# Attention in pairs of heads: where in the load queue a pair's values and the reciprocals of its sums stand

## The chip, the cores and the metric

The kernel runs on one core of a Trainium2 chip. The metric is the device time of one execution in microseconds (us), from the first to the last instruction and a little around them. The core has a matrix engine (TensorE, in the profile PE, its weight loads PEld), three elementwise engines (VectorE = DVE, ScalarE = ACT, GpSimd = POOL) and a sync engine (SP) that does nothing but issue transfers (DMAs). Each engine works through its own list of instructions in order. An instruction that waits for a semaphore holds up everything behind it on the same engine. That is also so on SP: a transfer that may not start yet holds up every later one.

## What is computed

Three layers follow one another; only the first is touched here.

```python
# B, H, S, D = 2, 8, 576, 64
scores = scale * np.matmul(q, k.transpose(0, 1, 3, 2))
...
bias = h @ w2                                   # a small net of the distance of two positions, one value per head
scores = scores + bias.transpose(2, 0, 1)[None, :, :, :]
scores = scores - np.max(scores, axis=-1, keepdims=True)
attn = np.exp(scores)
attn = attn / (np.sum(attn, axis=-1, keepdims=True) + 1e-09)
return np.matmul(attn, v).astype(np.float32)
# then  x = relu-like maximum of three products, times w_out   (1152 x 512 x 768)
# then  a mixture of 8 experts with balanced weights            (1152 x 512 x 1024 each)
```

## The kernel before

The program has these stages, in this order: the bias stage (0 to 70 us of the span), attention (68 to 216 us), the first product layer (the loop with `m1_mm`, to 326 us), then the experts to the end at 1082 us.

**Bias stage.** The bias of every head, row and column goes through a tensor in DRAM (`bias_f`). A loop over 36 groups `g16` of 16 rows makes each group on PE and DVE (`bias_mm`, `bias_ev`, `bias_out`), in one of six buffers `bo`, and `bias_store` writes it to DRAM. So the store of group n must have landed before `bias_out` of group n + 6 writes the buffer again. Behind groups 12, 20 and 28 `load_bias(0)` to `load_bias(2)` fetch the first bias tiles back, in the layout that attention wants.

**Attention.** The eight heads are taken in four pairs `p` (0 to 3), and a pair in nine steps `k` (0 to 8); step `s = 9p + k` of 36 handles 128 rows of queries of both heads `x`. In a step `u_qk` makes the scores on PE, `u_max` (L452, DVE, once per head) adds the bias tile and finds the row's extreme, `u_exp` (ACT) makes the exponentials and their sums, `u_tr` and `u_ev` transpose them (PE, then ACT and DVE). The product with the values, `pv_mm`, runs later: table `PV` gives pair p its parts at steps 9p + 5 to 9p + 13. A pair's values are therefore still read in the fifth step (k = 4) of the next pair, and first read in the sixth step (k = 5) of its own.

**The transfers of a pair.** All of them are issued by SP through the helper `dma` (L59), in the order in which the loop over `s` (L590 to L624) calls them:

- `load_pair(p + 1)` at k = 1: queries and keys of the next pair (two transfers of 576 KB into `qk`), then its values (640 KB into `v`). Both tiles have two buffers. The values of pair p + 1 go where those of pair p - 1 lie, and these are read by PE up to k = 4 of pair p.
- `load_bias(n)` at even k, with n = 5p + k/2 + 2: the bias tiles of both heads for row block n % 5 of pair n // 5, 288 KB each. There are six buffers, so tile n goes where tile n - 3 lay, which is read for the last time one step earlier. The tiles loaded at k = 2 (n = 5p + 3) are wanted by `u_max` at k = 6, those of k = 4 at k = 8, those of k = 6 and k = 8 at k = 0 and 2 of the next pair.
- the reciprocals of the sums: `r_add` at k = 0 forms them (DVE), `r_tr` and `r_out` at k = 1 write them to DRAM (`r_d`), `r_in` at k = 2 reads them back, spread over the partitions (four transfers, 576 KB in all, one buffer). `x_out` (POOL, called at k = 6 and 7) multiplies the finished rows of the pair before by them.
- `load_item`: weights of the first product layer, 512 KB each; `w_step` prepares them with DVE, ACT and POOL instructions spread over the steps `W_AT` of pairs 1 to 3.

In the source, `r_in` stands ahead of `load_bias` in a step, and `load_pair` behind it.

Of the kernel before, what the change touches and what calls it, by code (L numbers as in the profile page):

```python
# [9 lines left out]
F32 = mybir.dt.float32  # L10
# [10 lines left out]
B, H, S, D = 2, 8, 576, 64  # L21
# [30 lines left out]
def make_body(stop=None):  # L52
    def body(tc, a):
# [4 lines left out]
        def dma(out, in_):  # L58
            nc.sync.dma_start(out=out, in_=in_)  # L59
# [7 lines left out]
        def pool(name, bufs=1, space=None, side=None):  # L67
            kw = {}
            if space is not None:
                kw["space"] = space  # L70
            if side is not None:
                kw["side"] = side
            return tc.tile_pool(name=name, bufs=bufs, **kw)

        with ctx, tc.manual_schedule():
# [92 lines left out]
            hp_ = hctx.enter_context(pool("heads", bufs=2))  # L168

            qk_t, v_t = {}, {}  # L170
            bias_t = {}

            def load_pair(p):
                if p < H // 2:
                    qk_t[p] = hp_.tile([128, 2, B, S], F32, tag="qk", name="qk")
                    v_t[p] = hp_.tile([128, 2, B, 5, D], F32, tag="v", name="v")
                    for part in range(2):
                        dma(qk_t[p][:, part], a["qk"][p][:, part])
                    dma(v_t[p], a["v"][p])

            def load_bias(n):

                p, it = divmod(n, 5)
                for h in range(2 * p, 2 * p + 2) if n < 5 * H // 2 else ():
                    t = hp_.tile([128, S], F32, tag="bias", name="bias", bufs=6)
                    if it < 4:
                        dma(t, bias_d[128 * it:128 * it + 128, h, :])
                    else:
                        for e in range(2):
                            dma(t[64 * e:64 * e + 64], bias_d[512:576, h, :])  # L190
                    bias_t[h, it] = t


            with ExitStack() as bctx:
# [7 lines left out]
                dma(par, a["par"])  # L202
                nc.scalar.dma_start(out=rr, in_=a["tab4"])
                dma(tab16, a["tab16"])
                load_pair(0)
                w1r, b1r, w2r, msk, c4, wb1, w2a = (
                    par[:, i:j] for i, j in ((0, 1), (1, 2), (2, 10), (10, 42), (42, 186), (186, 250), (250, 506)))
                l16, ic16 = tab16[:, :TW], tab16[:, TW:]
# [20 lines left out]
                v, kf, po = (eu[:, i] for i in range(3))  # L229
# [77 lines left out]
                def gen_s(g):  # L307


                    n = width(g // 4)  # L310
                    s = sp.tile([128, 3, 194], F16, tag="s", name="s")[:, :, :n // 3]
                    win = v3(window(rs, g // 4))
                    kind = TESTS0[g] if g < len(TESTS0) else (TESTSL if g // 4 == NG16 - 1 else TESTS)[g % 4]
                    if kind == "A":
                        A.activation(out=s, in_=win, func=AF.Sigmoid, bias=nthr[:, g:g + 1], scale=STEEP)
                    else:
                        eng = G if kind == "G" else V
                        eng.tensor_scalar(out=s, in0=win, scalar1=thr[:, g:g + 1], scalar2=None, op0=ALU.is_gt)
                    s_t[g] = s
# [12 lines left out]
                def bias_mm(g16):  # L332
                    ps = []
                    for q in range(2):
                        pt, sls = sums(pb[q].tile([128, 2, 512], F32, tag="p", name="p"), width(g16))
                        ps.append(pt)
                        for p in range(2):
                            for sl in sls:
                                for c in range(4):
                                    T.matmul(out=pt[32 * c:32 * c + 32, sl, :], lhsT=wb[p][:, q, :],  # L340
                                             rhs=s_t[4 * g16 + c][:, sl, :], start=(p == 0), stop=(p == 1))
                    for c in range(4):
                        del s_t[4 * g16 + c]
                    return ps

                def bias_ev(g16, ps):
                    n = width(g16)
                    t = ev.tile([128, S], F32, tag="t", name="t")[:, :n]
                    V.scalar_tensor_tensor(out=v3(t), in0=ps[0], scalar=ics[:, g16:g16 + 1], in1=v3(window(l16, g16)),
                                           op0=ALU.mult, op1=ALU.mult)  # L350
                    return t
# [3 lines left out]
                def bias_out(g16, ps, t):  # L355
                    n = width(g16)
                    bo = bo_t[g16] = ev.tile([128, S + 24], F32, tag="bo", name="bo", bufs=6)
                    o = 16 * g16 + 15 if side(g16)[1] else 0
                    V.scalar_tensor_tensor(out=v3(bo[:, o:o + n]), in0=ps[1], scalar=sc[:, 1:2], in1=v3(t),  # L359
                                           op0=ALU.mult, op1=ALU.add)  # L360
# [17 lines left out]
                for g16 in range(NG16):  # L378
                    ps = bias_mm(g16)
                    t = bias_ev(g16, ps)  # L380
                    for c in range(4):
                        if g16 + 2 < NG16:
                            gen_s(4 * (g16 + 2) + c)
                    bias_out(g16, ps, t)
                    if g16 == NG16 - 1:

                        A.activation(out=bc.tile([128, 1], F32, name="ex"), in_=ones[:, 0:1], func=AF.Exp)
                    for n in range(max(g16 - 1, 0), NG16 if g16 == NG16 - 1 else g16):
                        bias_store(n)
                    if g16 in (12, 20, 28):  # L390
                        load_bias((12, 20, 28).index(g16))

            if stop == "bias":
                with pool("dbg") as dp:
# [15 lines left out]
            with ExitStack() as actx:  # L410
# [74 lines left out]
                def r_in(p):  # L485

                    r_t[0] = up.tile([128, B, S], F32, tag="r", name="r", bufs=1)
                    for x in range(2):
                        dma(r_t[0][half[x], :, 0:512], r_d[p, 9 * x:9 * x + 8, :].rearrange(
                            "(b t) p -> b (t p)", b=B).unsqueeze(0).to_broadcast([64, B, 512]))  # L490
                        dma(r_t[0][half[x], :, 512:576], r_d[p, 9 * x + 8, :].rearrange(
                            "(b p) -> b p", b=B).unsqueeze(0).to_broadcast([64, B, 64]))

                def u_tr(u, x):

                    pe = un[u]["pe"][x]
                    pt = un[u]["pt"] = ps_t.tile([128, 2, 512], F32, tag="pt", name="pt")
                    for j in range(5):
                        c = min(128 * j, S - 128)
                        for i in range(2):  # L500
                            T.transpose(pt[:, i, 64 * j:64 * j + 64], pe[half[i], c:c + 128], ident[half[i], half[i]])  # L501
# [76 lines left out]
                def in_turn(table, s):  # L578

                    return [(p, table[s - 9 * p]) for p in range(NP) if s - 9 * p in table]  # L580
# [9 lines left out]
                for s in range(NU):  # L590
                    p, k = divmod(s, 9)
                    u_qk(s)
                    if s > 0:
                        u_tr(s - 1, 0)
                    pv_part(s)
                    for x in range(2):
                        u_max(s, x)
                    if s > 0:
                        u_ev(s - 1, 0)
                    u_exp(s, 0)  # L600
                    for n, e in in_turn(EV, s):
                        pv_ev(n, *e)
                    u_exp(s, 1)
                    if s > 0:
                        u_tr(s - 1, 1)
                        u_ev(s - 1, 1)
                    if s > 8:
                        if k == 0:
                            r_add(p - 1)
                        if k == 1:  # L610
                            r_out(p - 1)
                        if k == 2:
                            r_in(p - 1)
                        if k in (6, 7):
                            x_out(p - 1, k - 6)
                        if k in W_AT:
                            w_step(last=2)
                    if s in (3, 7):
                        load_item(s // 4)
                    if s > 0 and (k == 0 or k % 2 == 0) and 5 * p + k // 2 + 2 < 5 * NP:  # L620
                        load_bias(5 * p + k // 2 + 2)
                    if k == 1:
                        load_pair(p + 1)
                    un.pop(s - 2, None)  # L624

                u = NU - 1
# [126 lines left out]
            with ExitStack() as mctx:  # L753
# [216 lines left out]
                for n, g in enumerate((0, 2, 1, 3)):  # L970
                    for d in range(4):
                        k = 4 * n + d
                        p = (ps_o, ps_o, ps_m, ps_m)[d].tile([128, 512], F32, tag="oomm"[d] + "2", name="o")
# [333 lines left out]
```

## Time and profile before

| | before |
|---|---|
| time, median of 3 runs | 1082.54 us (1078.12 to 1086.18) |
| profiled execution | 1084.35 us, of which 1082.6 us are the span |
| PE busy | 1049.3 us, 97% of the span |
| DVE, ACT, POOL busy | 755.8, 561.0, 313.3 us (70, 52, 29%) |
| mean granted TensorE clock | 0.984 of full speed |
| transfers of SP's queue | 83.81 MB, 27.2% of the 16 DMA engines' time |

The profile is of one execution. A busy share near 100% for PE does not say that nothing is lost: matmuls at a lower granted clock take longer and count as busy all the same, and a few us of waiting are well under 1% of the span. What the change is worth is read from the attention stage alone, from the queue of SP and from the engines that wait for its transfers.

### The profile page before, as it was taken

How to read it: one execution, taken by the hardware profiler on the slowest of the kernel's cores; microseconds unless marked ns; L12 is line 12 of the kernel's file. 1: busy time of each engine (PE TensorE's matmuls, PEld its weight loads, DVE VectorE, ACT ScalarE, POOL GpSimd, SP SyncE). 2: the span in 40 equal slices, each digit the busy share in tenths (PEclk: the TensorE clock that was granted, in tenths of full speed). 3: DMA queues.
4: the chain of work that ended last, by engine and by line, in shares of the span. 5: the costliest groups of instructions: out<-in, count | busy, mean ns of one | idle time of the engine just before them, and what ended most of it. 6: DMA issues, size and time to landing. Idle time of an engine off the chain costs nothing.

```text
span 1082.6 us, 18890 instructions
## 1 busy us (share of the span) xinstructions
PE 1049.3 (97%) x7533; PEld 686.5 (63%) x7533; DVE 755.8 (70%) x1464; ACT 561.0 (52%) x922; POOL 313.3 (29%) x227
## 2 busy tenths in 40 slices
PE   7989889999999999999999999999999999999998
PEld 3245455699999765665756657557566575665753
DVE  7977556599977877877667576676775666757543
ACT  6967566544434576454544545454445454454530
POOL 6830211322224224135141331322413314133120
PEclk8989898999999999999999999999999999999999
DMA  5884655243414013022130230211302203010002
GB/s 178 257 258 115 172 159 139 73 156 118 102 40 154 22 42 83 21 64 47 38 84 21 64 74 31 64 35 50 83 20 64 58 26 83 21 45 6 1 1 88
DMA packets 39446, 85.31 MB, mean 79 GB/s; under 512 B 8053, under 2 KB 10301, under 8 KB 39357
## 3 DMA queue, kind: packets, MB, share of 16 engines
q1 hardware_dynamic: 39212, 83.81, 27.2%
q8 instruction: 59, 0.97, 0.4%
q10 hardware_dynamic: 144, 0.29, 0.1%
q14 instruction: 31, 0.25, 0.1%
HBM read 70.78 MB, written 13.30 MB: 78 GB/s over the span
## 4 chain that ended last, share of the span: by engine, by line
PE 84%; DVE 9%; ACT 3%; DMA 3%; issue 1%; POOL 0%; SPq 0%; DVEq 0%; ACTq 0%
PE d L1211 32%; PE x L1126 12%; PE m L560 10%; PE y L1126 8%; PE z L1126 8%; PE pv L529 3%; PE sc L435 3%; PE pt L501 3%; PE p L340 2%; DVE bo L359 1%; DMA bias<-bias_f 1%; PE o L977 1%; DVE hl L1149 1%; DVE s L1140 1%; DVE pk L704 1%
## 5 line engine op out<-in xcount | busy, mean ns | idle before, releaser
L1211 PE MATMUL d<-w2h,hh 128*128 128x512 f16 x576 | 218.3, 379 | 0.8 <-DVE acc L1222 0.8
L1211 PE MATMUL d<-w2h,hl 128*128 128x512 f16 x576 | 218.3, 379 | 0.2 <-DVE hl L1149 0.2
L1211 PE MATMUL d<-w2l,hh 128*128 128x512 f16 x576 | 218.3, 379 | 0.0
L1126 PEld LDWEIGHTS <-w1h 128*128 128x128 f16 x1792 | 175.5, 98 | 49.8 <-issue 2.3
L1211 PEld LDWEIGHTS <-hh 128*128 128x128 f16 x1152 | 112.6, 98 | 132.9 <-issue 1.0
L1225 DVE SCALAR_TENSOR_TENSOR acc<-d,kh,acc 128x512 f32<-128x512 f32 x126 | 94.3, 748 | 93.7 <-PE d L1211 93.6
L857 POOL TENSOR_TENSOR w1l<-wf,w1h 128x768 f16<-128x768 f32 x32 | 53.6, 1677 | 360.2 <-ACT w1h L856 286.0
L1144 ACT ACTIVATE hh<-s 128x576 f16<-128x576 f32 x128 | 87.3, 683 | 128.6 <-DVE s L1140 100.9
L1149 DVE SCALAR_TENSOR_TENSOR hl<-s,hh 128x576 f16<-128x576 f32 x128 | 99.2, 777 | 48.4 <-ACT hh L1144 45.9
L863 POOL TENSOR_TENSOR w1l<-wf,w1h 128x1024 f16<-128x1024 f32 x32 | 68.8, 2152 | 117.6 <-ACT w1h L860 117.6
L860 ACT ACTIVATE w1h<-wf 128x1024 f16<-128x1024 f32 x32 | 33.8, 1056 | 132.5 <-DVE wf L853 132.5
L1126 PEld LDWEIGHTS <-w1l 128*128 128x128 f16 x896 | 87.9, 98 | 22.8 <-issue 0.4
L1211 PEld LDWEIGHTS <-hl 128*128 128x128 f16 x576 | 56.4, 98 | 68.5 <-DVE hl L1149 0.7
L1136 ACT ACTIVATE s<-x,cx 128x576 f32<-128x576 f32 x96 | 70.3, 733 | 27.0 <-PE x L1126 26.6
L938 POOL TENSOR_TENSOR w2l<-w2r,w2h 128x512 f16<-128x512 f32 x64 | 73.1, 1159 | 25.0 <-ACT w2h L937 25.0
L1126 PE MATMUL x<-xth,w1h 128*128 128x288 f16 x384 | 78.5, 286 | 0.6 <-ACT s L1136 0.6
L1126 PE MATMUL x<-xtl,w1h 128*128 128x288 f16 x384 | 78.6, 286 | 0.2 <-POOL xtl L868 0.2
L1126 PE MATMUL x<-xth,w1l 128*128 128x288 f16 x384 | 78.5, 286 | 0.0
L1140 DVE SCALAR_TENSOR_TENSOR s<-z,cx,s 128x576 f32<-128x576 f32 x64 | 52.3, 818 | 32.0 <-PE z L1126 25.6
L560 PE MATMUL m<-xh,wh 128*128 128x384 f32 x216 | 72.7, 337 | 0.0
L560 PE MATMUL m<-xl,wh 128*128 128x384 f32 x216 | 72.5, 336 | 0.1
L560 PE MATMUL m<-xh,wl 128*128 128x384 f32 x216 | 72.4, 335 | 0.0
(203 smaller groups left out, 1990.3 us busy)
## 6 DMA issues: line engine op xcount, KB each, us to landing
wr<-in_moe_w SPq DMA_DIRECT2D x50, 512.0 KB, 3.6
w2r<-in_moe_w SPq DMA_DIRECT2D x64, 256.0 KB, 2.9
bias_f<-bo SPq DMA_DIRECT2D x36, 295.5 KB, 3.6
bias<-bias_f SPq DMA_DIRECT2D x32, 288.0 KB, 4.6
qk<-in_qk SPq DMA_DIRECT2D x8, 576.0 KB, 5.8
wr<-in_moe_w_out SPq DMA_DIRECT2D x6, 512.0 KB, 4.1
v<-in_v SPq DMA_DIRECT2D x4, 640.0 KB, 4.3
bias<-bias_f SPq DMA_DIRECT2D x16, 144.0 KB, 5.8
```

Of the source, the lines that this page charges most:

```text
L560: T.matmul(out=p[:, :TG], lhsT=ws[:, 128 * c:128 * c + 128], rhs=xs[:, c, TG * g:TG * g + TG], start=(c == 0 and n == 0), stop=(c == 3 and ...
L857: G.tensor_tensor(out=lo[:, 0:3], in0=t[:, 1:4], in1=hi[:, 0:3], op=ALU.subtract)
L860: A.activation(out=hi[:, 3:7], in_=t[:, 4:8], func=AF.Copy)
L863: G.tensor_tensor(out=lo[:, 3:7], in0=t[:, 4:8], in1=hi[:, 3:7], op=ALU.subtract)
L938: G.tensor_tensor(out=lo, in0=r, in1=hi, op=ALU.subtract)
L1126: T.matmul(out=ps[bank][:, s, :SH], lhsT=ws[:, i, c, :], rhs=xv[:, j, c, s * SH:s * SH + SH], start=(start and k == 0), stop=(k == 5), **kw)
L1136: A.activation(out=t, in_=src, func=AF.Identity, scale=c)
L1140: V.scalar_tensor_tensor(out=out, in0=z, scalar=scale, in1=out, op0=ALU.mult, op1=ALU.add)
L1144: A.activation(out=o, in_=src, func=AF.Relu)
L1149: V.scalar_tensor_tensor(out=l, in0=src, scalar=0.0, in1=o, op0=ALU.max, op1=ALU.subtract)
L1211: T.matmul(out=pd, lhsT=hs[:, fh, 128 * t:128 * t + 128], rhs=ws, start=(k == 0), stop=(k == 11))
L1225: V.scalar_tensor_tensor(out=acc[:, t, :], in0=pd, scalar=kh[:, 1 + t:2 + t], in1=acc[:, t, :], op0=ALU.mult, op1=ALU.add)
```

## The change

`load_pair` is split in two. `load_qk` keeps the place of `load_pair` (before the bias stage for pair 0, at k = 1 for the next pair). `load_v` goes to k = 5, behind the bias tiles of k = 4; for pair 0 it goes into the bias stage, behind group 24. `r_in` stays at k = 2 but is called behind `load_bias` instead of ahead of it, and behind `w_step`. No instruction is added or removed; PE, DVE, ACT and POOL have the same instructions in the same order as before.

```diff
-            def load_pair(p):
+            def load_qk(p):
                 if p < H // 2:
                     qk_t[p] = hp_.tile([128, 2, B, S], F32, tag="qk", name="qk")
-                    v_t[p] = hp_.tile([128, 2, B, 5, D], F32, tag="v", name="v")
                     for part in range(2):
                         dma(qk_t[p][:, part], a["qk"][p][:, part])
+
+            def load_v(p):
+                if p < H // 2:
+                    v_t[p] = hp_.tile([128, 2, B, 5, D], F32, tag="v", name="v")
                     dma(v_t[p], a["v"][p])
...
-                load_pair(0)
+                load_qk(0)
...
                         load_bias((12, 20, 28).index(g16))
+                    if g16 == 24:
+                        load_v(0)
...
-                        if k == 2:
-                            r_in(p - 1)
...
                         load_bias(5 * p + k // 2 + 2)
+                    if k == 2 and p > 0:
+                        r_in(p - 1)
                     if k == 1:
-                        load_pair(p + 1)
+                        load_qk(p + 1)
+                    if k == 5:
+                        load_v(p + 1)
```

The first place is SP's queue from the start of the program through the bias stage. `qk` and `v` are the loads of pair 0, `bias_f<-bo` the stores of the groups, `bias<-bias_f` the first bias tiles; "x12" stands for twelve equal rows in a row.

```order
 L59 DMA qk<-in_qk 128x1152 x2
-L59 DMA v<-in_v 128x1280
 L59 DMA bias_f<-bo 16x8x591 x12
 L59 DMA bias<-bias_f 128x576 x2
 L59 DMA bias_f<-bo 16x8x591 x8
 L59 DMA bias<-bias_f 128x576 x2
-L59 DMA bias_f<-bo 16x8x591 x8
+L59 DMA bias_f<-bo 16x8x591 x4
+L59 DMA v<-in_v 128x1280
+L59 DMA bias_f<-bo 16x8x591 x4
 L59 DMA bias<-bias_f 128x576 x2
```

The values of pair 0 move from ahead of all stores to the middle of the third batch of eight stores, four stores ahead of the third pair of bias tiles.

The second place is SP's queue in pair 1, from its second step on: `r_d<-rt` writes the reciprocals of pair 0, `qk` and `v` are the loads for pair 2, `r<-r_d` reads the reciprocals back. The bias rows of 128 partitions are those of k = 2 (x2) and then of k = 6, 8 and the next k = 0 (x6), the rows of 64 partitions those of k = 4.

```order
 L59 DMA r_d<-rt 18x128
 L59 DMA qk<-in_qk 128x1152 x2
-L59 DMA v<-in_v 128x1280
+L59 DMA bias<-bias_f 128x576 x2
 L59 DMA r<-r_d 64x2x512
 L59 DMA r<-r_d 64x2x64
 L59 DMA r<-r_d 64x2x512
 L59 DMA r<-r_d 64x2x64
-L59 DMA bias<-bias_f 128x576 x2
 L59 DMA bias<-bias_f 64x576 x4
+L59 DMA v<-in_v 128x1280
 L59 DMA bias<-bias_f 128x576 x6
```

The two bias tiles of k = 2 now stand directly behind the queries and keys, the reciprocals behind them, and the values behind the bias tiles of k = 4. Pair 2 changes in the same way (with a load of weights ahead of the two bias tiles), pair 3, which has no next pair to load, only in that the reciprocals stand behind the two bias tiles.

## Rows read from the trace of the kernel before

**Rows 1.** The page's part 4, the chain that ended last, by engine and by line.
```profile
PE 84%; DVE 9%; ACT 3%; DMA 3%; issue 1%; POOL 0%; SPq 0%; DVEq 0%; ACTq 0%
PE d L1211 32%; PE x L1126 12%; PE m L560 10%; PE y L1126 8%; PE z L1126 8%; PE pv L529 3%; PE sc L435 3%; PE pt L501 3%; PE p L340 2%; DVE bo L359 1%; DMA bias<-bias_f 1%; PE o L977 1%; DVE hl L1149 1%; DVE s L1140 1%; DVE pk L704 1%
```

**Rows 2.** Busy time by stretch, attention: length, engines' busy us, granted clock, DMA share, GB/s.
```profile
99.00:116.60 17.60, 17.60 (x195) 10.79 (x195) 12.24 (x29) 13.50 (x31) 0.00 (x0) 1.00 0.31 96
116.60:125.00 8.40, 4.88 (x64) 3.02 (x63) 2.96 (x7) 3.13 (x7) 1.32 (x1) 1.00 1.03 275
125.00:134.30 9.30, 7.58 (x58) 4.39 (x60) 5.04 (x11) 3.95 (x9) 5.61 (x6) 0.63 0.47 131
...
175.00:191.80 16.80, 16.80 (x184) 9.84 (x185) 12.27 (x29) 13.09 (x30) 0.00 (x0) 1.00 0.48 138
191.80:201.00 9.20, 9.20 (x124) 5.68 (x124) 6.87 (x16) 6.80 (x16) 8.21 (x7) 1.00 0.06 23
```

**Rows 3.** Timeline of DVE in attention: start, us, instruction, idle before it and releaser.
```profile
116.63 0.76 DVE L452 CUSTOM_DVE_ANT_0 ng<-sc,bias 128x576 f32<-128x576 f32 x1 [0.30 <-PE sc L435]
...
119.25 0.68 DVE L128 SCALAR_TENSOR_TENSOR ww<-wr,ww 128x512 int32<-128x512 int32 x1
124.90 0.76 DVE L452 CUSTOM_DVE_ANT_0 ng<-sc,bias 128x576 f32<-128x576 f32 x1 [4.97 <-DMA bias<-bias_f]
...
134.33 0.76 DVE L452 CUSTOM_DVE_ANT_0 ng<-sc,bias 128x576 f32<-128x576 f32 x1
...
154.46 0.76 DVE L452 CUSTOM_DVE_ANT_0 ng<-sc,bias 128x576 f32<-128x576 f32 x1
...
157.08 0.42 DVE L125 TENSOR_SCALAR ww<-ww 128x512 int32<-128x512 int32 x1
...
171.68 0.76 DVE L452 CUSTOM_DVE_ANT_0 ng<-sc,bias 128x576 f32<-128x576 f32 x1 [0.73 <-PE sc L439]
...
191.81 0.76 DVE L452 CUSTOM_DVE_ANT_0 ng<-sc,bias 128x576 f32<-128x576 f32 x1 [0.30 <-PE sc L435]
...
200.94 0.76 DVE L452 CUSTOM_DVE_ANT_0 ng<-sc,bias 128x576 f32<-128x576 f32 x1 [0.40 <-PE sc L439]
```

**Rows 4.** Timeline of SP in pairs 1 and 3: start, us of issuing, transfer, count.
```profile
106.33 1.67 SPq L59 DMA_DIRECT2D qk<-in_qk  x2
115.05 0.33 SPq L59 DMA_DIRECT2D v<-in_v  x1
115.47 2.57 SPq L59 DMA_DIRECT2D r<-r_d  x4
118.08 18.04 SPq L59 DMA_DIRECT2D bias<-bias_f  x12
...
182.17 2.56 SPq L59 DMA_DIRECT2D r<-r_d  x4
184.82 3.49 SPq L59 DMA_DIRECT2D bias<-bias_f  x6
```

**Rows 5.** SP's own waits, 60 to 220 us: whom for, total, times, longest.
```profile
SPq L59 <- PE pv L529: 15.4, 2, 8.5
```

**Rows 6.** Tile bias, transfers issued 121 to 122.5 us: time to landing.
```profile
DMA to landing us min/median/max: 7.4/7.4/7.4
```

**Rows 7.** Busy time by stretch, bias stage (columns as in rows 2).
```profile
51.00:59.00 8.00, 7.81 (x94) 1.94 (x95) 8.00 (x17) 7.86 (x17) 7.97 (x6) 1.00 0.84 250
```

**Rows 8.** Tile bo: stores issued 53.0 to 56.0 us, their landing; the store at 35.6.
```profile
L59 SPq DMA_DIRECT2D bias_f<-bo x3: 518/518/518, 53.0 to 56.0; - x3
...
DMA to landing us min/median/max: 3.1/3.2/3.3
...
DMA to landing us min/median/max: 6.8/6.8/6.8
```

**Rows 9.** The chain that ended last, in order of time: start, us, what.
```profile
59.86 0.71 DVE bo L359
```

**Rows 10.** POOL's timeline: the multiplication that reads the reciprocals of pair 0.
```profile
123.68 1.40 POOL L544 TENSOR_TENSOR x<-x,r 128x576 f32<-128x576 f32 x1 [60.56 <-DMA r<-r_d]
```

## The prediction

> **What bounds the kernel now.** I read the chain that ended last first [rows 1]. PE has 84% of it, nearly all in the two later layers, which the change does not touch. One entry does not belong to a stage that PE bounds: 1% of the chain, some 11 us, is a transfer, the loads of bias tiles, and such a load exists only in the bias stage and attention. So I went to the attention stage by stretches [rows 2]. In the first half of pair 1 (99.0 to 116.6) and of pair 3 (175.0 to 191.8) PE is busy for all of the stretch at a granted clock of 1.00, the 2.4 GHz level: PE is the bound there, and the work goes at its best pace. Between 116.6 and 125.0 PE is busy for 4.88 of 8.40 us and the transfers take all there is (share 1.03, 275 GB/s). Behind it, from 125.0 to 134.3, PE gets a clock of 0.63, a mix of the two levels. The same steps of pair 3 (191.8 to 201.0) have PE busy for 9.20 of 9.20 us at 1.00.
>
> DVE's timeline says who stood still [rows 3]. The instruction of the seventh step of pair 1 (k = 6) starts at 124.90, after 4.97 us of idling for a bias tile. SP's timeline says why the tile was late [rows 4]: the queries and keys are issued by 108.0, then nothing until the values go out at 115.05, the reciprocals take until 118.04, and only then, at 118.08, the two bias tiles go that are wanted from about 119.6 on. What the values waited for is in SP's own waits [rows 5]: twice for PE's product with the values, 15.4 us in all. That is the buffer: the old values are read by PE up to the fifth step. So the wait is real, but it is the values' own, and the bias tiles merely stand behind them. Pair 3 has no values to load: its reciprocals go out at 182.17, its bias tiles at 184.82 [rows 4], and DVE's idling there is a few tenths for PE.
>
> **What the change costs and saves, part by part.**
>
> *Values at k = 5, bias tiles of k = 2 ahead of them.* The loss is the time from DVE's instruction of k = 5 to that of k = 8 in a pair, against pair 3, where the same steps run without a stall [rows 3]. Pair 1: 134.33 - 116.63 = 17.70 us. Pair 2: 171.68 - 154.46 = 17.22 us. Pair 3: 200.94 - 191.81 = 9.13 us. The excess is 8.57 + 8.09 = 16.66 us. It holds the wait itself (about 5 us each), PE's low clock behind it, and the refilling of the steps. I take pair 3 as what pairs 1 and 2 become, for the matmuls of these steps are the same and PE was already full in pair 3, so they cannot become much faster.
>
> *One difference between the pairs.* In pairs 1 and 2 weight preparation falls into these steps on DVE: one instruction of 0.68 us at 119.25 (hidden in the stall), its like at k = 7, and one of 0.42 us in pair 2 [rows 3]. Nothing of them is hidden by a stall any more; what hides them is DVE's slack, 9.20 - 6.87 = 2.33 us over three steps [rows 2], 0.78 each. They cost between nothing and their sum of 0.68 + 0.68 + 0.42 = 1.78 us. The slack lies in two pieces per step, so I take a third, 0.6 us. The saving is 16.66 - 0.6 = 16.1 us.
>
> *Are the tiles in time in the new place?* They follow the queries and keys directly, at 108.0 and some 0.6 us later, since the tile they overwrite was read one step before. The slowest landing of a bias tile in attention was 7.4 us [rows 6], with the DMA engines full. That gives 116.0 against 119.6, a margin of 3.6 us. By bytes: two loads of 576 KB and two of 288 KB are 1.77 MB, at 275 GB/s [rows 2] 6.4 us from 106.33, or 112.8 before the landing's own delay. Cost nothing; if a row three times as slow existed it would be a stall again, and that is a rival below.
>
> *Reciprocals behind the bias tiles.* They still go some 6 us earlier than now (about 109.2 against 115.47 [rows 4]). Who waits for them is POOL, which began at 123.68 after 60.56 us of idling [rows 10], and nothing but the layer behind attention and the next `r_in` waits for POOL. Queued behind them on SP are the bias tiles of k = 4, wanted at k = 8, some 14 us later. Cost nothing in pairs 1 and 2. In pair 3 they move from 182.17 to behind two issues of about 0.6 us; the multiplications are called four steps later. Cost nothing.
>
> *The values at k = 5.* They are issued when PE has finished with the old ones, as now, at about 115.05. They are first read nine steps after k = 5, some 29 us later. Behind them stand the bias tiles of k = 6, released at about 118 by DVE and wanted at the next k = 0, about 128.7 (134.33 - 8.57 + 2.9): with 7.4 us of landing 125.5, a margin of 3 us. Cost nothing.
>
> *Values of pair 0 in the bias stage.* 640 KB join a stretch in which the transfers already take 0.84 of the DMA engines [rows 7]. DVE is busy for 8.00 of 8.00 us there and is the bound, so the transfer costs only if a store lands too late for its buffer. The store that goes out at 53.0 lands in 3.1 to 3.3 us [rows 8], and the buffer is written again six groups on, at 59.86 [rows 9]: it has 6.86 us. The store at 35.6, directly behind two bias tiles of together 576 KB, took 6.8 us [rows 8]. So the cost lies between nothing and 655,360 bytes at 275 GB/s, 2.4 us, if the stage became bound by transfers. I take nothing, since the nearest row fits into its time by a hair. Leaving the start of the program frees nothing: the tables that DVE waits for are issued ahead of the values.
>
> The Trainium skill ("DMA: Bandwidth & Descriptors", Rules for kernel authors) says that to overlap a transfer with work one issues it early, computes, and waits for it late. By that rule moving the values to a later step gives up cover, and the sum would be no gain. This trace disagrees with it for this queue: issued early in the program, the values went out at 115.05 all the same, and took 6.9 and 8.5 us of everyone else's time.
>
> *The sum* against the profiled execution: 1084.35 - 16.1 = 1068.3 us. That execution lies 1.8 us above the median of the runs shown, so against the median it is 1082.54 - 16.1 = **1066.4 us**, I say 1066.5. The stages behind attention wait for attention's end and for PE, so they start earlier and keep their length. Where the stall goes: the next to be late is PE itself.
>
> **Rivals.**
>
> *A stall stays in one of the two pairs, or half in both.* The bias tiles of k = 2 then land late behind the queries and keys, in pair 2 also behind 512 KB of weights. It decides from a landing of about 11 us on (119.6 - 108.6). Against it is the margin above; for it, that transfers do fill the engines in a burst (share 1.03). It would give back some 8.3 us: 1074.7.
>
> *The bias stage becomes bound by transfers.* Worked out above, 2.4 us: 1068.9. Against it is DVE's 8.00 of 8.00. The same page (Issuing engines are not separate DMA queues) says that all transfers share the same 16 engines and interleave, so a load moved into a full stretch takes from the others. The landing of 6.8 us beside 3.1 to 3.3 agrees.
>
> *Nothing happens.* The tiles would have to be held by something else than the values, such as their own buffer. That was free since step k = 1, and SP's wait names PE: 1082.5.
>
> *Slower.* `r_in` needs POOL to have finished with the single buffer of reciprocals. If POOL were late, SP would stand at `r_in`, and behind it the bias tiles of k = 4 and the values, in pairs 2 and 3. To end 1% above before, the two pairs must lose the 16.1 us gained and 10.8 more, 13.5 us each; with the 14 us until those tiles are wanted POOL would have to be some 27 us late, at `r_in` of pair 1's sums (about 139). POOL's start goes from 123.7 to about 116, so it is early. It would give 1093 or more.
>
> **How the numbers follow.** My forecast 0.80, transfers bound in the bias stage 0.05, a stall that stays 0.08, nothing 0.04, slower 0.03. The first two are faster by over 1% (10.8 us, about what a measurement of this kernel can tell from no change): 0.85. A stall that stays saves 7.8 us, under 1%; with nothing that is 0.12. Slower 0.03. The range: upward to the stall that stays, 1074.5, which takes in both bounds, 1.2 us for DVE's preparation and 2.4 us for the bias stage. Downward the whole 16.66 us give 1065.9, and one run lay 4.4 us under the median before, so 1061.
>
> **What would show it.** In the changed kernel's profile SP should not wait for PE's product between the queries and the bias tiles of k = 2; DVE's instruction of k = 6 should idle for tenths in all pairs; the times from k = 5 to k = 8 should be 9.1 to 9.8 us in pairs 1 and 2; the granted clock should be 1.00 through pairs 1 to 3 and its mean about 0.99; attention should end some 16 us earlier, and the layers behind it keep their length. A stretch of 0.6 in the clock, or DVE idling for a bias tile, would prove the forecast wrong, and DVE waiting for a store in groups 29 to 31 would show the cost in the bias stage.

## The result, and the profile after

The changed kernel takes 1068.46 us, the median of four runs (1065.98 to 1070.50), against 1083.70 for four of the kernel before: ratio 0.9865, 95% interval 0.9819 to 0.9912. It was run twice more beside the experiments, at 0.9845 (0.9811 to 0.9878) and 0.9852 (0.9830 to 0.9873). One of the nine executions of the kernel before in the last series took 5433.85 us and is left out of every ratio and difference. The forecast was 1066.5 us with a range of 1061 to 1074.5. The profiled execution took 1065.98 us, of which the span is 1064.2.

The chain by engine answers to [rows 1]: the entry of DMA falls from 3% to 1%, and the load of bias tiles is no longer among the lines shown.

```profile
PE 85%; DVE 9%; ACT 3%; DMA 1%; issue 1%; POOL 0%; DVEq 0%; ACTq 0%
PE d L1218 33%; PE x L1133 12%; PE m L565 11%; PE y L1133 8%; PE z L1133 8%; PE pv L534 4%; PE sc L440 3%; PE pt L506 3%; PE p L343 1%; DVE bo L362 1%; PE o L984 1%; DVE s L1147 1%; DVE hl L1156 1%; DVE pk L711 1%; DMA bias_f<-bo 1%
```

By stretches (length, then busy us of PE, PEld, DVE, ACT, POOL, granted clock, DMA share, GB/s), cut at pairs 1, 2 and 3. This answers to [rows 2].

```profile
96.60:126.70 30.10, 30.10 (x343) 18.97 (x344) 23.22 (x51) 22.82 (x51) 7.28 (x6) 1.00 0.59 175
126.70:156.50 29.80, 29.80 (x346) 18.18 (x345) 21.88 (x49) 22.53 (x51) 8.29 (x7) 1.00 0.66 206
156.50:183.00 26.50, 26.50 (x315) 16.21 (x315) 19.57 (x45) 20.00 (x45) 8.19 (x7) 1.00 0.34 100
```

PE is busy all the time at a clock of 1.00 through three pairs; the stretches at 0.6 are gone. SP's timeline in pair 1 (start, us of issuing, transfer) answers to [rows 4].

```profile
103.80 1.66 SPq L59 DMA_DIRECT2D qk<-in_qk  x2
105.55 0.86 SPq L59 DMA_DIRECT2D bias<-bias_f  x2
106.50 3.21 SPq L59 DMA_DIRECT2D r<-r_d  x4
109.81 4.30 SPq L59 DMA_DIRECT2D bias<-bias_f  x4
114.82 0.33 SPq L59 DMA_DIRECT2D v<-in_v  x1
115.25 10.76 SPq L59 DMA_DIRECT2D bias<-bias_f  x6
```

The two bias tiles of k = 2 go out directly behind the queries and keys, 105.55 - 103.80 = 1.75 us after them; in the kernel before it was 118.08 - 106.33 = 11.75 us [rows 4]. The landing that the profile shows for them took 7.0 us, so they were there at about 113; DVE used the first at 118.02.

```profile
DMA to landing us min/median/max: 7.0/7.0/7.0
```

The wait of SP for PE's product with the values [rows 5] has no row any more. DVE's timeline in pairs 1 and 2 answers to [rows 3].

```profile
114.09 0.76 DVE L457 CUSTOM_DVE_ANT_0 ng<-sc,bias 128x576 f32<-128x576 f32 x1 [0.30 <-PE sc L440]
...
116.72 1.38 DVE L128 SCALAR_TENSOR_TENSOR ww<-wr,ww 128x512 int32<-128x512 int32 x1
118.02 0.74 DVE L457 CUSTOM_DVE_ANT_0 ng<-sc,bias 128x576 f32<-128x576 f32 x1
...
126.73 0.76 DVE L457 CUSTOM_DVE_ANT_0 ng<-sc,bias 128x576 f32<-128x576 f32 x1 [0.29 <-ACT pe L467]
...
144.07 0.76 DVE L457 CUSTOM_DVE_ANT_0 ng<-sc,bias 128x576 f32<-128x576 f32 x1
...
146.70 1.23 DVE L125 TENSOR_SCALAR ww<-ww 128x512 int32<-128x512 int32 x1
...
156.55 0.76 DVE L457 CUSTOM_DVE_ANT_0 ng<-sc,bias 128x576 f32<-128x576 f32 x1 [0.29 <-PE sc L440]
```

From k = 5 of a pair to k = 0 of the next is 126.73 - 114.09 = 12.64 us in pair 1 and 12.48 in pair 2; before it was 20.63 and 20.16. The idling for a bias tile is gone. Two of the preparation instructions shown have become longer, 1.38 against 0.68 us and 1.23 against 0.42; more on them below.

Where did the 18.4 us by which the two spans differ come from? DVE's first instruction of attention starts 1.27 us earlier (69.23 against 70.50), the first nine steps take 27.40 against 28.68 us (1.28), the steps from the tenth to the last 86.26 against 101.76 (15.50), and what follows 881.31 against 881.66 (0.35). The 15.50 are the change. The first two are not, as the experiments show.

The table holds the median of every kernel that was run, its ratio to the kernel before in the same series, and the times between DVE's first score instructions of two steps in its profile: the first nine steps, the two pairs from k = 5 to the next k = 0, and the tenth to the last step; with the granted clock from 68 to 79 us.

| kernel | median us, ratio | first 9 steps | clock 68 to 79 | pair 1 | pair 2 | 10th to last step |
|---|---|---|---|---|---|---|
| before | 1083.70 | 28.68 | 0.53 | 20.63 | 20.16 | 101.76 |
| changed | 1068.46, 0.9865 | 27.40 | 0.84 | 12.64 | 12.48 | 86.26 |
| changed, 2nd time | 1066.06, 0.9845 | 28.84 | 0.54 | 12.08 | 12.10 | 85.15 |
| changed, 3rd time | 1068.74, 0.9852 | 32.83 | 0.50 | 12.87 | 12.07 | 86.10 |
| values alone moved | 1069.23, 0.9857 | 32.84 | 0.57 | 13.03 | 12.06 | 86.07 |
| reciprocals alone moved | 1072.25, 0.9889 | 28.84 | 0.53 | 12.56 | 15.58 | 89.54 |
| before, third values buffer | 1069.99, 0.9865 | 28.83 | 0.53 | 17.47 | 12.71 | 91.14 |
| values at k = 3 | 1066.08, 0.9827 | 26.32 | 1.00 | 12.08 | 12.06 | 85.13 |
| preparation early | 1066.67, 0.9846 | 30.13 | 0.52 | 11.85 | 12.06 | 85.13 |
| values at 3, preparation early | 1066.73, 0.9843 | 31.42 | 0.54 | 11.85 | 12.06 | 85.10 |
| one matmul more per bank | 1063.92, 0.9824 | 26.32 | 1.00 | 13.12 | 12.06 | 86.17 |
| the same again | 1063.90, 0.9818 | 31.76 | 0.69 | 12.72 | 12.86 | 86.70 |
| the same, and five at the end | 1064.08, 0.9811 | 26.32 | 1.00 | 12.74 | 12.07 | 85.79 |

### The profile page after: what moved, and what is told of

Its sections match the earlier page's. It is cut to its first block, busy times and chain, and to the rows that moved or that the text cites. A ratio compares the mean times of both kernels' runs of the same rounds, so it can differ in the third digit from the quotient of the medians.

```text
span 1064.2 us, 18893 instructions
## 1 busy us (share of the span) xinstructions
PE 1040.0 (98%) x7533; PEld 682.8 (64%) x7533; DVE 756.7 (71%) x1464; ACT 560.8 (53%) x922; POOL 313.7 (29%) x227
## 4 chain that ended last, share of the span: by engine, by line
PE 85%; DVE 9%; ACT 3%; DMA 1%; issue 1%; POOL 0%; DVEq 0%; ACTq 0%
PE d L1218 33%; PE x L1133 12%; PE m L565 11%; PE y L1133 8%; PE z L1133 8%; PE pv L534 4%; PE sc L440 3%; PE pt L506 3%; PE p L343 1%; DVE bo L362 1%; PE o L984 1%; DVE s L1147 1%; DVE hl L1156 1%; DVE pk L711 1%; DMA bias_f<-bo 1%
```

## Experiments: which part of the queue made the tiles late

Theory Q is that of the prediction: the tiles stand behind the values, which wait for their buffer. Theory B is its rival: the tiles are late since values, reciprocals and tiles leave in one burst that fills the DMA engines (share 1.03 in [rows 2]).

**Only the values moved.** In the changed kernel, `r_in` goes back to its old place.

```diff
+                        if k == 2:
+                            r_in(p - 1)
...
-                    if k == 2 and p > 0:
-                        r_in(p - 1)
```

> Only the values are moved (k = 5, pair 0 behind group 24); the reciprocals stay ahead of the bias tiles of k = 2. I measure a pair by the time from DVE's score instruction of k = 5 to that of the next pair's k = 0: 20.63 us in pair 1 and 20.16 in pair 2 before, 12.64 and 12.48 in the changed kernel. Theory Q (the tiles stand behind the values, which wait for their buffer): the tiles go out behind 2.6 us of issuing the reciprocals, about 109.5 us instead of 105.5, land by 117 and are wanted at about 117: 12.5 to 13.5 us per pair, ratio to before within 0.002 of the changed kernel's 0.9865. Theory B (the tiles are late since values, reciprocals and tiles leave in one burst that fills the DMA engines): the reciprocals' part of the burst stays ahead of the tiles, 14 to 16 us per pair, ratio 0.990 to 0.995.

Measured: 0.9857 (0.9831 to 0.9883), pairs of 13.03 and 12.06 us. Moving the values alone brings the whole gain, as Q says and B does not. The reciprocals ahead of them delay the tiles: they are issued at 113.00, 4.13 us behind the queries and keys (1.75 in the changed kernel). They land in 5.4 us and still come in time: DVE idles for no tile in pair 1. What pair 1 has above pair 2 is a preparation instruction of DVE, 1.78 us instead of 0.68, beside one of POOL's; more on such pairs below.

```profile
121.79 1.78 DVE L128 SCALAR_TENSOR_TENSOR ww<-wr,ww 128x512 int32<-128x512 int32 x1
123.49 0.74 DVE L457 CUSTOM_DVE_ANT_0 ng<-sc,bias 128x576 f32<-128x576 f32 x1
```

The fence is DVE's timeline of this kernel (start, us): the score instruction of the next step stands directly behind the stretched one.

**Only the reciprocals moved.** In the kernel before, `r_in` goes behind `load_bias`; the values stay at k = 1.

```diff
-                        if k == 2:
-                            r_in(p - 1)
...
+                    if k == 2 and p > 0:
+                        r_in(p - 1)
                     if k == 1:
                         load_pair(p + 1)
```

> Only the reciprocals are moved behind the bias tiles of k = 2; the values stay at k = 1, ahead of both, in every pair. Theory Q: the tiles still go out only when the values' buffer is free, but 2.6 us of issuing earlier (about 115.5 instead of 118.1); DVE still idles 2 to 3 us in pairs 1 and 2, 17 to 18.5 us per pair against 20.63 and 20.16, total 4 to 6 us under before. Theory B: the tiles now share the burst with the values alone, land 3 us sooner besides, and most of the loss is gone: 13 to 15 us per pair, 11 to 14 us under before.

Measured: 0.9889 (0.9865 to 0.9914), some 12 us gained; pairs of 12.56 and 15.58 us. Q as I had put it is wrong here, and B's forecast of 11 to 14 us came out: SP waits for PE as long as before, and most of the loss is gone all the same. SP's waits (whom for, total, times, longest), its timeline in pair 1, DVE's timeline in pairs 1 and 2, and a stretch of pair 2 (columns as above):

```profile
SPq L59 <- PE pv L529: 15.3, 2, 8.6
```

```profile
113.83 0.33 SPq L59 DMA_DIRECT2D v<-in_v  x1
114.25 0.86 SPq L59 DMA_DIRECT2D bias<-bias_f  x2
115.20 2.57 SPq L59 DMA_DIRECT2D r<-r_d  x4
```

```profile
118.63 0.75 DVE L452 CUSTOM_DVE_ANT_0 ng<-sc,bias 128x576 f32<-128x576 f32 x1
...
150.19 0.76 DVE L452 CUSTOM_DVE_ANT_0 ng<-sc,bias 128x576 f32<-128x576 f32 x1 [1.55 <-DMA bias<-bias_f]
```

```profile
153.30:158.20 4.90, 4.90 (x52) 2.96 (x50) 2.27 (x5) 2.78 (x6) 3.42 (x3) 0.65 1.03 276
```

The tiles go out right behind the values at 114.25, and DVE uses the first at 118.63, 4.4 us later, without idling, so it had landed by then; in the kernel before, with the reciprocals ahead, the tile issued at 118.08 was used at 124.90, 6.8 us later. So the reciprocals cost twice: 2.6 us of issuing ahead of the tiles, and at least 6.8 - 4.4 = 2.4 us of the tiles' landing. In pair 2 the weights' 512 KB stand ahead of the tiles besides, the tile takes 6.1 us, DVE idles 1.55 us for it, PE's clock is 0.65 for some 5 us, and the pair takes 3.5 us more than the 12.06 of a pair without loss.

**The old order with a third buffer for the values.** It takes away what the load waits for, and nothing else.

```diff
-                    v_t[p] = hp_.tile([128, 2, B, 5, D], F32, tag="v", name="v")
+                    v_t[p] = hp_.tile([128, 2, B, 5, D], F32, tag="v", name="v", bufs=3)
```

> The order of before, all of it, but a third buffer for the values, so that their load at k = 1 has no reader to wait for. Theory Q: SP no longer waits for PE, the tiles go out at about 111 us and land in time or a little late: 12.1 to 13.5 us per pair, 14 to 17 us under before. Theory B: queries, keys, values, reciprocals and tiles (about 3 MB) now leave in a single burst, longer than before, and the tiles are late again: 15 to 18 us per pair, less than 10 us under before.

Measured: 0.9865 (0.9838 to 0.9892), 14 us gained; pairs of 17.47 and 12.71 us. No wait of SP for PE is left. Queries, keys, values, reciprocals and tiles go out one behind the other from 105.38 to 112.4, the tiles from 111.19. The chain that ended last (start, us) and DVE's timeline in pair 1, and the stretches (columns as above):

```profile
111.19 9.03 DMA bias<-bias_f
```

```profile
120.39 0.76 DVE L452 CUSTOM_DVE_ANT_0 ng<-sc,bias 128x576 f32<-128x576 f32 x1 [1.41 <-DMA bias<-bias_f]
122.14 0.76 DVE L452 CUSTOM_DVE_ANT_0 ng<-sc,bias 128x576 f32<-128x576 f32 x1 [0.98 <-ACT pe L462]
```

```profile
115.60:120.40 4.80, 4.80 (x64) 3.07 (x64) 2.88 (x7) 3.18 (x7) 1.26 (x1) 1.00 1.06 199
120.40:124.40 4.00, 2.31 (x14) 1.45 (x11) 2.26 (x5) 1.74 (x4) 3.73 (x5) 0.78 0.90 221
124.40:130.20 5.80, 5.80 (x51) 3.13 (x51) 2.96 (x7) 2.22 (x5) 1.94 (x2) 0.56 0.40 113
```

The tile took 9.0 us to land in pair 1 and 10.2 in pair 2, more than any in the kernel before, with the DMA share at 1.06. In pair 1 DVE idled only 1.41 us for it, but PE then stood for 1.7 us in two pieces, its clock fell to 0.56, near the 1.2 GHz level, and the pair lost 17.47 - 12.06 = 5.4 us. That is B's mechanism, in one pair of two: pair 1 lies in B's 15 to 18 us, pair 2 in Q's 12.1 to 13.5, and the 14 us gained at the lower end of Q's 14 to 17.

Both theories are therefore half right. A tile was late by the sum of three things ahead of it: the values' wait for their buffer (6.9 to 8.5 us), the issuing of the reciprocals (2.6 us), and a landing that grows from some 4 to 10 us with what was issued just before. Take the first or the second away and it comes in time, or nearly.

**The values two steps earlier.** In the changed kernel `load_v` is called at k = 3.

```diff
-                    if k == 5:
+                    if k == 3:
                         load_v(p + 1)
```

> The changed kernel with the values at k = 3 instead of k = 5, so behind the tiles of k = 2 and the reciprocals but ahead of the tiles of k = 4. SP still stands at the values until PE has read the old ones (about 115 us), and the tiles of k = 4 wait behind them. Theory Q, with time to spare as its measure: those tiles are wanted at k = 8 (about 124), and from 115 on they land by 122.5: no stall, 12.5 to 13 us per pair, the changed kernel's time within 2 us. If instead any wait on SP in these steps costs what it lasts, the 4 to 5 us of waiting show in each pair: 16 to 17 us, ratio 0.995.

Measured: 0.9827 (0.9800 to 0.9853), pairs of 12.08 and 12.06 us, below the 12.5 to 13 expected. SP now does wait for PE:

```profile
SPq L59 <- PE pv L534: 6.7, 2, 4.1
```

Nobody loses by these 6.7 us, since the tiles behind go out at 111.55 and 140.83 and are wanted some 10 us later. In these runs a wait on SP cost only what it exceeded the time that the transfers behind it had to spare. The median is lower than the changed kernel's, but the steps are not: 85.13 us from the tenth to the last, 85.15 in the changed kernel's second profile. The difference lies ahead of them, in the clock of the first steps.

## Experiments: what is left in the pairs

Without any loss pairs 1 and 2 take 12.06 us. The changed kernel's three profiles have 12.08 to 12.87 in pair 1 and 12.07 to 12.48 in pair 2, together 0.06 to 1.00 us more than twice 12.06. In each of them one of DVE's preparation instructions, or one of POOL's, is stretched. POOL's timeline of the changed kernel, first and second profile, has at the same place:

```profile
116.14 1.41 POOL L549 TENSOR_TENSOR x<-x,r 128x576 f32<-128x576 f32 x1 [53.30 <-DMA bias<-bias_f]
```

```profile
117.93 1.96 POOL L549 TENSOR_TENSOR x<-x,r 128x576 f32<-128x576 f32 x1 [55.81 <-ACT pe L467]
```

DVE's timeline of the second profile:

```profile
117.94 0.68 DVE L128 SCALAR_TENSOR_TENSOR ww<-wr,ww 128x512 int32<-128x512 int32 x1
```

In the first, POOL began at 116.14, DVE's L128 at 116.72 took 1.38 us instead of 0.68: it ended 0.55 us after POOL's. In the second both began within 0.01 us, DVE's took 0.68 and POOL's 1.96 instead of 1.41. One of the two is not disturbed, and the times of the other fit a wait for it; where the starts lie clearly apart, it is the first to begin that keeps its time.

**Preparation in steps 0 to 4**, where none of POOL's multiplications falls.

```diff
-W_AT = (0, 2, 4, 5, 7)
+W_AT = (0, 1, 2, 3, 4)
```

> The changed kernel with weight preparation in steps k = 0 to 4 of pairs 1 to 3 instead of k = 0, 2, 4, 5 and 7. In the changed kernel three of DVE's preparation instructions took 1.38, 1.02 and 1.23 us where they fell beside POOL's two-operand instructions, against 0.68, 0.68 and 0.42 elsewhere. Theory P (they share something with POOL, and the stretched instruction delays the score instruction behind it): none of them falls beside POOL now, each takes 0.4 to 0.7 us, and pairs 1 and 2 take 12.1 to 12.2 us as pair 3's pace gives; 1 us less in total. Rival: DVE's own slack is what lacks, wherever they stand: the same 0.5 us per pair are lost at another k, time as the changed kernel.

Measured: 0.9846 (0.9810 to 0.9883). L128 and L130 take 0.68 us, L124 and L125 0.42, POOL's two-operand instructions on 128x576 tiles 1.40 to 1.42, every one of them: theory P. Pairs 11.85 and 12.06 us, 85.13 from the tenth to the last step. That is what the changed kernel has when the meetings cost it nothing (85.15, its second profile), so it removes a loss of up to 1.1 us. Pair 1 takes 17.67 us from k = 0 to k = 5 instead of 17.45, and gets that back in the 11.85, so no loss has moved to the earlier steps. In the time of whole executions nothing shows: 1066.67 against 1066.06 us of the changed kernel beside it.

**Both.** The values at k = 3 and the preparation in steps 0 to 4.

```diff
-W_AT = (0, 2, 4, 5, 7)
+W_AT = (0, 1, 2, 3, 4)
...
-                    if k == 5:
+                    if k == 3:
                         load_v(p + 1)
```

> Values at k = 3 (the previous experiment's fastest) and weight preparation in steps 0 to 4 together. With the values at k = 3 pairs 1 and 2 took 12.08 and 12.06 us already, so theory P expects nothing more from the preparation: 12.0 to 12.2 us per pair, and the time of the kernel with values at k = 3, ratio 0.982 to 0.985. If preparation in the earlier steps costs PE time there, k = 0 to 4 of pair 1 get longer than the 17.5 us they took.

Measured: 0.9843 (0.9815 to 0.9871), 85.10 us from the tenth to the last step, 17.67 us from k = 0 to k = 5. Nothing is added, as expected, and the ratio lies in the 0.982 to 0.985 that were expected.

The Trainium skill ("SBUF — State Buffer", SBUF: two separate sides) says that VectorE and GpSimd share a port pair under an exclusive lock, taken by whichever starts first for its whole instruction, among others by a VectorE instruction with two operands in SBUF. The rows agree: 0.68 against 1.38 us for such an instruction beside POOL's, and 1.41 against 1.96 the other way round. The one-operand L125, 0.42 against 1.23 us, agrees if it ran in one of the modes that the page counts in; no row here shows the mode.

## Experiments: the clock at attention's start

Three profiles of one and the same changed kernel have 27.40, 28.84 and 32.83 us for its first nine steps, at clocks of 0.84, 0.54 and 0.50 from 68 to 79 us. PE has gaps there: before attention in the last bias groups, and in the first steps, which have no product with values yet.

**The changed kernel a second and a third time.**

> The changed kernel once more, unchanged, beside the next three on one chip. Both theories: pairs 1 and 2 as before in it, 12.6 and 12.5 us from k = 5 to the next k = 0; ratio to before 0.985 to 0.988. What is open is the stretch from 68 to 79 us: in the six profiles so far the granted clock there was 0.53, 0.84, 0.57, 0.53, 0.53 and 1.00, and the first six steps took 17 to 24 us. If that differs between executions of one kernel, this run's clock there will not be the changed kernel's 0.84, and the time will follow it: 1.3 us more at 0.53.

> The changed kernel a third time, beside the next two, in more executions. Theory C (the clock of attention's first steps differs between executions, and most of the spread of the times with it): granted clock from 68 to 79 us of 0.5 to 1.0 in the profile, first nine steps of 26 to 32 us, times of 1064 to 1071 us, the lower ones those with the higher mean clock. From the tenth step to the last 85.1 to 86.3 us, as in its two profiles so far, whatever the clock ahead was.

Measured: 1066.06 and 1068.74 us. Pairs and later steps repeat within 1.1 us; the first steps do not. The times follow the mean clock: 1064.98 us at 0.993 and 1071.33 at 0.985 are the ends of one series of four. Of what was expected, "1.3 us more at 0.53" came near (28.84 against 27.40), while the second profile's pairs, 12.08 and 12.10 us, are better than the 12.6 and 12.5 foretold; the third profile's 32.83 us lie just above the 26 to 32 foretold, since the clock of about 0.5 lasted to about 90 us there: 5.4 us more than in the first.

**One more matmul per bank in bias groups 26 to 35**, its result never used: the real work overwrites it or does not read it.

```diff
-                        pt, sls = sums(pb[q].tile([128, 2, 512], F32, tag="p", name="p"), width(g16))
+                        tile_ = pb[q].tile([128, 2, 512], F32, tag="p", name="p")
+                        pt, sls = sums(tile_, width(g16))
+                        if g16 >= 26:
+                            T.matmul(out=tile_[:, 1, :], lhsT=wz[:, :128], rhs=wz, start=True, stop=True)
```

> The changed kernel with one more matmul (128 x 512, its result thrown away, 0.2 to 0.25 us) ahead of each bank's work in bias groups 26 to 35, so that PE is busier ahead of attention. Theory C (the clock that the first steps of attention get depends on how busy PE was in the groups before): PE busy 8 of the 9 us from 59 to 68 instead of 6.6, granted clock 0.9 to 1.0 from 68 to 79, the first six steps 17 us, time 2 to 4 us below the changed kernel, spread of the runs smaller. Rival: the added matmuls delay DVE, which bounds the bias stage, or the clock falls anyway for the idling inside the first steps: attention begins 1 to 3 us later, same clock of 0.5 to 0.8, time equal or up to 3 us worse.

> The kernel with one more matmul per bank in bias groups 26 to 35 again, in more executions: its four times so far were 1063.2, 1063.8, 1064.1 and 1068.5 us at mean clocks of 0.997, 0.996, 0.995 and 0.988. Theory C: most executions again at a mean clock of 0.995 or more and 1063 to 1064 us, a few at 0.988 and 1068; the median 1.5 to 4 us below the changed kernel's beside it. Rival: the three were chance, as one execution of another kernel with 0.997 was, and the medians are within 1 us.

Measured: 0.9824 (0.9794 to 0.9854) and 0.9818 (0.9792 to 0.9844), medians of 1063.92 and 1063.90, 2.1 and 4.8 us below the changed kernel beside it. Of nine executions seven were at a mean clock of 0.994 to 0.997 and 1062.8 to 1065.4 us, two at 0.988 and 0.989 and 1068.5 and 1069.5. One of those two was profiled: 0.69 from 68 to 79 us, 31.76 for the first nine steps. None of the changed kernel's 13 executions reached 0.994 (0.985 to 0.993); of the twelve with the values at k = 3, the preparation early or both, two did. So the odds shift, and the low clock remains possible.

**And five more matmuls behind the last group**, in the gap ahead of attention's first scores.

```diff
+                    if g16 == NG16 - 1:
+                        fill = pb[0].tile([128, 2, 512], F32, tag="p", name="p0")
+                        for _ in range(5):
+                            T.matmul(out=fill[:, 1, :], lhsT=wz[:, :128], rhs=wz, start=True, stop=True)
```

> The same with five more such matmuls behind the last group, where PE idles for 1.5 us before attention's first scores (busy 1.46 of the 2 us from 66 to 68 with one per bank, 0.2 to 0.8 without). Theory C: no execution at 0.988 any more, granted clock 1.00 from 68 to 79, all times within 1062.5 to 1065 us, since attention begins at the same time, bound by DVE. Rival: the five matmuls wait for their bank and hold up the first scores behind them, attention begins 0.5 to 1.5 us later, and the times are those of the kernel with one per bank plus as much.

Measured: 0.9811 (0.9794 to 0.9827), 1064.08 us; all five executions between 1063.32 and 1064.98 at a mean clock of 0.995 to 0.997. The stretches from 59 to 68 and from 68 to 79 us, of the changed kernel beside it first, then of this one:

```profile
59.00:68.00 9.00, 6.64 (x130) 3.51 (x127) 8.39 (x13) 6.34 (x13) 3.04 (x2) 0.93 0.78 246
68.00:79.00 11.00, 8.48 (x57) 6.06 (x56) 5.29 (x14) 4.99 (x12) 0.00 (x0) 0.50 0.80 261
```

```profile
59.00:68.00 9.00, 8.94 (x159) 3.83 (x149) 8.39 (x13) 6.32 (x13) 3.80 (x3) 1.00 0.80 252
68.00:79.00 11.00, 7.63 (x88) 4.99 (x89) 7.44 (x18) 7.21 (x17) 0.00 (x0) 1.00 0.80 264
```

PE is busy for 8.94 instead of 6.64 of the nine us, DVE for the same 8.39, so the bias stage is no longer; the clock stays at 1.00 and more steps fit into the next eleven us. Attention starts at 69.11 against 69.47, so the matmuls hold up nothing. This kernel is faster by 1.9% than before, and by 4.7 us in the median than the changed kernel beside it. From the one without the five it is not told apart: 1064.08 against 1063.90 us, and five of five executions at the high clock against four of five beside it.

## Why the prediction was right, and where it was not

*The size.* 16.1 us were forecast for pairs 1 and 2. The steps from the tenth to the last took 101.76 us before and 86.26, 85.15 and 86.10 in three profiles after: 15.5 to 16.6 us gained. Taking pair 3 as what the others become was the right template. By the prediction's own measure, k = 5 to k = 8, pairs 1 and 2 took 10.15 and 9.53, 9.44 and 9.15, 10.37 and 9.12 us against 17.70 and 17.22, so 15.2, 16.3 and 15.4 us were saved; pair 1 lies above the 9.8 us foretold in two profiles of three. The whole executions gained 15.2, 18.3 and 15.9 us in the medians, spread by the clock of the first steps. That the first series came within 2 us of 1066.5 is in part luck: that clock alone moved the first steps by up to 5.4 us between executions, and the sum has no term for it.

*The cause.* "It is the values' own wait, and the bias tiles merely stand behind them" was too simple. With the wait in place and the reciprocals out of the way 12 us came back; with the wait removed and the order kept 14. What the prediction left out is that the landing depends on what was issued just before. Its 7.4 us [rows 6] came close in the changed kernel, where the tiles of k = 2 in pair 1 took 7.0, 7.6 and 7.1 us in the three profiles, with some five us to spare in the first. It is not a bound: the third buffer showed 9.0 and 10.2. The rival "a stall stays in one of the two pairs" did not happen here, but did in two experiments, one pair each, at 3.5 and 5.4 us instead of the 8.3 priced.

*Preparation on DVE.* 0.6 us were taken, between 0 and 1.78; the two pairs together lost 0.06 to 1.00 in the three profiles against 12.06 each, and 0.3 to 1.4 by the prediction's own measure. The size was about right, the reason not: it is not that DVE's slack is too small, but that POOL's multiplications fall beside it. With the preparation away from them, in steps 0 to 4, nothing is lost.

*Reciprocals behind the tiles.* POOL was to begin at about 116; it began at 116.14, and no engine waits for its multiplications in attention.

*Values of pair 0 in the bias stage.* Nothing was taken, and nothing is seen that they cost: from 51 to 59 us DVE is busy for 8.00 of 8.00 us in the changed kernel's second and third profile. In the first it is 7.64, where a store landed after 6.89 us and DVE idled 0.36; that store was issued at 46.12, behind two bias tiles, but was still under way when these values went out at 50.30. So a cost of 0.4 us in that one profile is not ruled out; the 2.4 us of the rival did not come. The 1.27 us by which attention began earlier are no gain of the change either: with the values of pair 0 at the old place, two experiments began at 69.12 and 69.39, and the 70.50 of the kernel before holds a store's delay of its own.

*The rule on early issue.* The prediction set this rule of the Trainium skill ("DMA: Bandwidth & Descriptors", Rules for kernel authors) against the trace, and the measurement decides: the values alone, issued four steps later, made the kernel 1.4% faster, and at k = 3 or 5 there is no difference in the pairs. Issued early into a third buffer they made it 1.4% faster too, with 5.4 us lost to the burst in pair 1. So what early issue cost here came for the most part from standing ahead of a buffer that was not free.

*Left open.* What decides in a single execution whether the clock falls at attention's start was not settled, only that filling PE's gaps ahead of it kept it up in five of five executions. The gap alone does not tell: PE stands 1.77 us ahead of the first scores in all three profiles of the changed kernel (clock 0.84 to 0.50 behind it) and as long in that with the values at k = 3 (1.00). No experiment made shorter gaps in attention's middle.

## What to carry to other kernels

In a queue that issues in order, put a transfer that has to wait for its buffer behind those that are free to go, near the step in which the buffer comes free; left ahead, it costs at least what its wait exceeds the time that the transfers behind it have to spare. When a tile is late, add up everything ahead of it (waits, issuing, bytes in flight), since removing any one part may be enough, and removing the wait alone may turn it into a burst. A stall of PE cost more than it lasted, most of the rest through the clock behind it: 1.7 us of standing and 5.4 lost with the third buffer (5.80 us of work at 0.56), 5.2 us of standing in pair 1 before and 8.6 lost (7.58 us of work at 0.63, [rows 2]). So closing a small gap in attention's middle was worth more than its length.

## What the runs showed that was not expected

- The clock of attention's first steps is not the same in every execution of one kernel: the changed kernel's first nine steps took 27.4 to 32.8 us in three profiles, at granted clocks of 0.84 to 0.50 from 68 to 79 us, and the same steps 26.3 at 1.00 in other kernels. By these profiles it is most of the changed kernel's spread of 1065 to 1071 us. With 25 matmuls of thrown-away work five executions lay within 1.7 us.
- A bias tile of 288 KB landed in 2.8 us with no other load issued just ahead of it, and in 10.2 at the end of 3 MB and more issued within some 7 us.
- DVE's 0.68 us instruction took up to 1.87 us beside POOL's, and POOL's 1.41 up to 1.96 beside DVE's.
